# Attention with fp32 products with v, the last 64 keys mixed once, and odd scores copied by VectorE

## The chip, the core and the metric

The kernel runs on one core of a Trainium2 chip. Its time is the device time of one execution in microseconds (us). Before the change three runs gave a median of 881.18 us (880.06 to 882.84). One more execution was profiled; it took 882.68 us, and all rows below are from it.

## The reference

Attention for 4 batches, 12 heads, 448 positions and head size 64 is mixed over heads twice, before and after the softmax; two gated dense blocks follow, which the change does not touch.

```
scores = q @ k.T / sqrt(64)
scores = einsum('bhij,hg->bgij', scores, w_pre)      # heads mixed: premix
attn = exp(scores - max); attn /= sum + 1e-9
attn = einsum('bhij,hg->bgij', attn, w_post)         # heads mixed: postmix
x = attn @ v                                         # then moe, then moe2
```

## The kernel before

Attention comes first and the dense part after it; all instructions of an engine run in the order in which the program lists them, and the loop in `attention` (L438) writes that order by hand.

**Tiles and steps.** The 448 queries of a batch are cut into tiles of 120, 120, 120 and 88. A block is 10 queries of all 12 heads, that is 120 rows, laid out in two halves of the 128 partitions, five queries in each half. A step r takes two blocks; the tile of 88 ends with an odd step of one block of 8 queries. There are 23 steps a batch and 92 in all.

**What a step lists.** `relayout` (L230) copies scores into block layout by DMA on SP's queue, four steps ahead. `postmix(r)` (L288) multiplies the exponentials of the step by the weights `wr`, on tiles of 64x64 of the array: for each block e, each of four groups of 128 keys, both halves of the keys and both halves h of the rows. The keys are 448, so the fourth group overlaps the third by 64 keys. `recip2` and `weigh` (L267, L274) prepare the weights of step r+1 on VectorE and GpSimd. `at_hi` (L319, ScalarE) and `at_lo` (L327, VectorE) split the mixed result in PSUM into two fp16 parts `ah` and `al` for each block. Then come `scores` for a later tile (L202), `premix(r+2)`, its row maximum on VectorE, its exponential on ScalarE and a sum's reciprocal (L238 to L265), then `at_lo` of the second block, and then the step's unit of `attn_v` (L339), when there is one, and `out_x` (L357), which moves a finished half tile out of PSUM for `store_x`.

**The products with v.** `attn_v(b, t, c)` makes one pair of heads for one tile of queries. It sums twelve fp16 terms for each of the two heads: for four groups of keys, v high by `ah`, v high by `al` and v low by `ah`. A tile has six such units, one a step in most steps; two share a step once for the first tile and once for the third tile of each batch, and three share each of two steps for the last tile.

**Preparing v.** v is loaded in four parts a batch (`load_v`). VectorE takes its largest magnitude for each head pair (`v_max`, `v_join`), two small products on TensorE spread it over the partitions (`v_turn`, `v_spread`, which use the scores' PSUM tile psA), VectorE makes a power of two from it (`v_scale`), GpSimd multiplies (`v_mul`), VectorE casts to fp16 (`v_hi`) and GpSimd subtracts to get the low part (`v_lo`), one head pair a step over six steps. `out_x` multiplies by the inverse scale.

**PSUM.** psA is one tile of two banks for scores, psB two banks for premix, psC three banks for postmix and, for odd c of the first two tiles (`apart`, L209), for scores; psD is one bank for attn_v.

Between these, 18 jobs that decode the first dense weight (L575 to L628) put work on ScalarE, VectorE and GpSimd in steps 8 to 85, in the lists `mid` and `late` of the loop.

Of the kernel before, what the change touches and what calls it, by code (L numbers as in the profile page):

```python
# [17 lines left out]
NP = H // 2  # L18
# [3 lines left out]
TB = 8  # L22
# [4 lines left out]
QCOLS = [p + NP * n for p, (t0, n) in zip(SKIP, TILES)]  # L27
LR, LQ = 4, 2
# [3 lines left out]
EXP_BITS = 0x7F800000  # L32


def attention(tc, nc, io, xT, B, extra, tail):
# [16 lines left out]
    with ExitStack() as es:  # L52
# [21 lines left out]
        vsc_p = pool("a_vsc", 2)  # L74
# [4 lines left out]
        def pow2(out_scale, out_inv, mx, n):  # L79

            nc.vector.tensor_scalar(out=mx, in0=mx, scalar1=2.0 ** -100, scalar2=None, op0=ALU.max)
            e = sm_p.tile([128, n], F32, tag="p2e", name="p2e", bufs=1)
            f = sm_p.tile([128, n], F32, tag="p2f", name="p2f", bufs=1)
            nc.vector.tensor_scalar(out=e.bitcast(I32), in0=mx.bitcast(I32), scalar1=EXP_BITS,
                                    scalar2=None, op0=ALU.bitwise_and)
            nc.vector.tensor_scalar(out=f.bitcast(I32), in0=e.bitcast(I32), scalar1=EXP_BITS,
                                    scalar2=None, op0=ALU.bitwise_xor)
            nc.vector.tensor_scalar(out=out_scale, in0=f, scalar1=2.0 ** 13, scalar2=None, op0=ALU.mult)
            nc.vector.tensor_scalar(out=out_inv, in0=e, scalar1=2.0 ** -14, scalar2=None, op0=ALU.mult)

# [8 lines left out]
        KINDS = (SQ, TB)  # L99
        wts = {n: cp.tile([128, H, n], F32, name=f"w{n}") for n in KINDS}  # L100
# [3 lines left out]
        dwp = cp.tile([128, NP], F32, name="dwp")  # L104
        ident = cp.tile([128, 128], F32, name="ident")
        ones = cp.tile([NP, 128], F32, name="ones")

        def consts():
            o = 0
            for n in KINDS:  # L110
                nc.sync.dma_start(out=wts[n], in_=io["kpost"][:, H * o:H * (o + n)].rearrange("p (g i) -> p g i", g=H))
                o += n
            nc.sync.dma_start(out=ident, in_=io["ident"])
            nc.vector.memset(ones, 1.0)
            wrep = e_p.tile([128, S], F32, tag="e", name="wrep")[:, :H * H].rearrange("p (g h) -> p g h", g=H)
            nc.sync.dma_start(out=wrep, in_=io["w_postT"].rearrange("g h -> (g h)").partition_broadcast(128)
                                .rearrange("p (g h) -> p g h", g=H))
            mx = sm_p.tile([128, H], F32, tag="wmx", name="wmx", bufs=1)
            nc.vector.tensor_reduce(out=mx, in_=wrep, axis=AX.X, op=ALU.max, apply_absolute_value=True)
            sw = sm_p.tile([128, H], F32, tag="sw", name="sw", bufs=1)  # L120
            dw = sm_p.tile([128, H], F32, tag="dw", name="dw", bufs=1)
            pow2(sw, dw, mx, H)
            for n in KINDS:
                nc.vector.tensor_tensor(out=wts[n], in0=wts[n], in1=sw.unsqueeze(2).to_broadcast([128, H, n]),
                                        op=ALU.mult)
            for e in range(2):
                nc.vector.tensor_scalar(out=dwp[64 * e:64 * e + 64], in0=dw[64 * e:64 * e + 64, e::2],
                                        scalar1=8.0, scalar2=None, op0=ALU.mult)


        raws, kt, qt = {}, {}, {}
# [10 lines left out]
        vt, dsc = {}, {}  # L142

        vraw = vr_p.tile([128, 4, NP, 128], F32, name="vraw")
        nc.gpsimd.memset(vraw[:64, 3], 0.0)

        def load_v(b, j):
            p = slice(0 if j < 3 else 64, 128)
            nc.sync.dma_start(out=vraw[p, j], in_=io["vN"][b, 128 * j:min(128 * j + 128, S)].rearrange("p (c d) -> p c d", d=128))

        def v_max(b, j):
            if j == 0:
                raws["vmx", b] = sm_p.tile([128, 4, NP], F32, tag="vmx", name="vmx", bufs=1)
            nc.vector.tensor_reduce(out=raws["vmx", b][:, j], in_=vraw[:, j], axis=AX.X, op=ALU.max,
                                    apply_absolute_value=True)

        def v_join(b):
            mx = raws["vmx", b]
            m = raws["vmx", b] = sm_p.tile([128, NP], F32, tag="vmj", name="vmj", bufs=1)
            nc.vector.tensor_reduce(out=m, in_=mx.rearrange("p j c -> p c j"), axis=AX.X, op=ALU.max)  # L160

        def v_turn(b):

            ps = raws["vps", b] = psA.tile([128, 2, 512], F32, tag="psA", name="psV")[:, 0]
            nc.tensor.matmul(ps[:NP, :128], raws.pop(("vmx", b)), ident, start=True, stop=True)

        def v_top(b):
            m = sm_p.tile([NP, 1], F32, tag="vtop", name="vtop", bufs=1)
            nc.vector.tensor_reduce(out=m, in_=raws.pop(("vps", b))[:NP, :128], axis=AX.X, op=ALU.max)
            dg = raws["dg", b] = sm_p.tile([NP, NP], F32, tag="dg", name="dg", bufs=1)  # L170
            nc.vector.tensor_scalar(out=dg, in0=ident[:NP, :NP], scalar1=m, scalar2=None, op0=ALU.mult)

        def v_spread(b):

            ps = raws["vps", b] = psA.tile([128, 2, 512], F32, tag="psA", name="psV")[:, 0]
            nc.tensor.matmul(ps[:, :NP], ones, raws.pop(("dg", b)), start=True, stop=True)

        def v_scale(b):
            mx, dv = (sm_p.tile([128, NP], F32, tag=t, name=t, bufs=1) for t in ("vm", "dv"))
            nc.vector.tensor_copy(mx, raws.pop(("vps", b))[:, :NP])  # L180
            sv = raws["sv", b] = vsc_p.tile([128, NP], F32, tag="sv", name="sv")
            pow2(sv, dv, mx, NP)
            dsc[b] = vsc_p.tile([128, NP], F32, tag="dsc", name="dsc")
            nc.vector.tensor_tensor(out=dsc[b], in0=dv, in1=dwp, op=ALU.mult)

        def v_mul(b, c):
            raw = vraw[:, :, c]
            nc.gpsimd.tensor_scalar(out=raw, in0=raw, scalar1=raws["sv", b][:, c:c + 1], scalar2=0.0,  # L188
                                    op0=ALU.mult, op1=ALU.add)

        def v_hi(b, c):
            vt[b, c] = [v_p.tile([128, 4, 128], F16, tag=f"{t}{c}", name=t) for t in ("vh", "vl")]
            nc.vector.tensor_copy(vt[b, c][0], vraw[:, :, c])

        def v_lo(b, c):
            vh, vl = vt[b, c]
            nc.gpsimd.tensor_tensor(out=vl, in0=vraw[:, :, c], in1=vh, op=ALU.subtract)  # L197
# [4 lines left out]
        def scores(b, t, c):  # L202
# [58 lines left out]
        def recip(r):  # L261
            m, sm = len(ex[r]), rec[r]
            rc = rec[r] = sm_p.tile([128, 2], F32, tag="rc", name="rc")
            nc.gpsimd.tensor_scalar(out=rc[:, :m], in0=sm[:, :m], scalar1=1e-9, scalar2=2.0 ** -14,  # L264
                                    op0=ALU.add, op1=ALU.mult)  # L265
# [5 lines left out]
        def kind(r):  # L271
            return SQ if pairs[r][4] == 2 else pairs[r][5]

        def weigh(r):  # L274
            n, rc = kind(r), rec.pop(r)
            wr[r] = []
            for e in range(len(ex[r])):
                w = wr_p.tile([128, H, IB], F32, tag="wr", name="wr")
                w = w.rearrange("p g i -> p (g i)")[:, :H * n].rearrange("p (g i) -> p g i", i=n)
                nc.gpsimd.tensor_scalar(out=w, in0=wts[n], scalar1=rc[:, e:e + 1], scalar2=0.0,  # L280
                                        op0=ALU.mult, op1=ALU.add)
                wr[r].append(w)

        def keys(x, jc):
            j0 = min(128 * jc, S - 128)
            return x[:, j0:j0 + 128]

        def postmix(r):  # L288
            n = kind(r)
            pc[r] = [psC.tile([128, 4, H, IB], F32, tag="psC", name="psC") for _ in ex[r]]  # L290
            if n != SQ:
                for ps, x, w in zip(pc[r], ex[r], wr[r]):
                    for jc in range(4):
                        nc.tensor.matmul(ps[:, jc, :, :n], keys(x, jc), w, start=(jc == 0), stop=(jc == 3))
# [1030 lines left out]
```

## Time and profile before

| | us |
|---|---|
| median of three runs | 881.18 |
| profiled execution | 882.68 |
| its span | 880.9 |
| TensorE (PE) busy in the span | 847.7 |
| VectorE (DVE) busy | 659.0 |
| ScalarE (ACT) busy | 534.7 |
| GpSimd (POOL) busy | 253.4 |

Busy time is a sum over stages with different limits, and TensorE's products are pipelined, so that their recorded durations overlap. What a product costs is read from the distance to the start of the next one. The granted clock of TensorE was full (2.4 GHz) but for the first microseconds: 0.997 over the span.

### The profile page before, as it was taken

The numbers are of one execution on the slowest core, as the hardware profiler recorded it, in microseconds if no ns is written. First come the engines' busy times: TensorE is split into PE (matmuls) and PEld (weight loads), VectorE is DVE, ScalarE is ACT, GpSimd is POOL, SyncE is SP. The second block draws the span as 40 slices with busy tenths as digits, with TensorE's granted clock in tenths as the row PEclk, the third lists the DMA queues.
The fourth block names the chain that finished last, engine by engine and source line by source line (L and its number), as shares of the span: only waits on it lengthen the run. The fifth ranks groups of instructions, "written<-read, shape, count | busy, mean of one in ns | idle before, by whom it ended". The sixth has DMA issues, their size and how long they took to land.

```text
span 880.9 us, 29335 instructions
## 1 busy us (share of the span) xinstructions
PE 847.7 (96%) x12008; PEld 672.5 (76%) x12008; DVE 659.0 (75%) x1471; ACT 534.7 (61%) x1202; POOL 253.4 (29%) x453
## 2 busy tenths in 40 slices
PE   8898899989999999999999999999999999999998
PEld 2455556656666666788998989898999999999997
DVE  3787888888889888879999998969886368338221
ACT  5788788978898898865656857327535136115010
POOL 0173146224522452100000000017417128306321
PEclk9999999999999999999999999999999999999999
DMA  6566555765576554652585957997530311310301
GB/s 206 171 202 207 166 168 189 236 183 168 175 244 188 161 176 145 183 162 83 155 270 169 295 170 227 326 331 239 193 110 12 115 36 37 115 28 1 108 19 63
DMA packets 108998, 141.70 MB, mean 161 GB/s; under 512 B 25792, under 2 KB 95168, under 8 KB 108864
## 3 DMA queue, kind: packets, MB, share of 16 engines
q1 hardware_dynamic: 108864, 139.82, 50.1%
q8 instruction: 95, 1.56, 0.7%
q14 instruction: 39, 0.32, 0.1%
HBM read 73.66 MB, written 27.59 MB: 115 GB/s over the span
## 4 chain that ended last, share of the span: by engine, by line
PE 70%; DVE 11%; ACT 5%; DMA 5%; POOL 4%; issue 4%; SPq 1%; POOLq 0%; ACTq 0%; DVEq 0%
PE ps L554 47%; PE psC L302 7%; PE psB L244 5%; PE psA L219 5%; PE psD L354 5%; POOL vl L197 2%; DMA wth<-wth_d 2%; ACT e L258 1%; ACT s L225 1%; DVE nmx L250 1%; DMA blk<-s 1%; DVE al L331 1%; POOL wr L280 1%; DMA xres<-xT 1%; POOL vraw L188 1%
## 5 line engine op out<-in xcount | busy, mean ns | idle before, releaser
L258 ACT ACTIVATE e<-psB,nmx 128x448 f32<-128x448 f32 x180 | 112.9, 636 | 36.2 <-DVE nmx L250 35.5
L331 DVE SCALAR_TENSOR_TENSOR al<-psC,ah 128x480 f16<-128x480 f32 x180 | 116.0, 645 | 13.0 <-ACT ah L325 12.1
L302 PE MATMUL psC<-wr,e 64*64 64x60 f32 x5632 | 107.2, 222 | 12.0 <-issue 9.1
L250 DVE TENSOR_REDUCE nmx<-psB 128x1 f32<-128x448 f32 x180 | 103.7, 616 | 17.8 <-PE psB L244 16.2
L302 PEld LDWEIGHTS psC<-wr,e 64*64 64x64 f32 x5632 | 94.0, 135 | 25.5 <-issue 11.4
L550 POOL TENSOR_TENSOR x2s<-x,x2s 128x384 fp32r<-128x384 f32 x28 | 28.8, 1047 | 283.1 <-DMA x2T<-xres 207.9
L244 PE MATMUL psB<-blk,kpre 64*64 64x448 f32 x720 | 102.9, 548 | 1.6 <-DMA blk<-s 0.8
L554 PE MATMUL ps<-wtok,z 128*128 128x448 f32 x504 | 104.3, 367 | 0.0
L325 ACT ACTIVATE ah<-psC 128x480 f16<-128x480 f32 x180 | 93.7, 579 | 15.6 <-PE psC L302 15.3
L554 PEld LDWEIGHTS ps<-wtok,z 128*128 128x128 f32 x504 | 94.6, 188 | 9.0
L219 PE MATMUL psA<-k,q 64*64 64x448 f32 (+2 forms) x768 | 94.4, 545 | 6.2 <-ACT s L225 5.2
L354 PEld LDWEIGHTS <-vh 128*64 128x64 f16 x1536 | 56.4, 110 | 56.9 <-issue 56.7
L554 PE MATMUL ps<-wth,x2s 128*128 128x384 f32 x504 | 94.2, 342 | 2.5 <-POOL x2s L550 1.9
L554 PEld LDWEIGHTS ps<-wth,x2s 128*128 128x128 f32 x504 | 88.1, 188 | 4.1 <-POOL x2s L550 2.9
L554 PE MATMUL ps<-u,wch 128*128 128x448 f32 x432 | 89.5, 367 | 0.0
L225 ACT ACTIVATE s<-psA 124x896 f32<-124x896 f32 (+1 forms) x90 | 84.1, 935 | 8.7 <-PE psA L219 5.9
L554 PEld LDWEIGHTS ps<-u,wch 128*128 128x128 f32 x432 | 81.1, 188 | 7.6
L550 POOL TENSOR_TENSOR z<-zz,z 128x384 fp32r<-128x384 f32 x56 | 64.3, 1169 | 55.7 <-ACT z L547 55.6
L547 ACT ACTIVATE u<-xres 128x448 fp32r<-128x448 f32 x24 | 13.8, 577 | 98.8 <-DVE xres L1133 98.8
L264 POOL TENSOR_SCALAR rc<-sum 128x2 f32<-128x2 f32 (+1 forms) x92 | 22.3, 243 | 174.2 <-ACT e L258 173.0
L244 PEld LDWEIGHTS psB<-blk,kpre 64*64 64x64 f32 x720 | 37.2, 132 | 44.5 <-issue 22.3
L280 POOL TENSOR_SCALAR wr<-w,rc 128x60 f32<-128x60 f32 x180 | 54.2, 314 | 55.6 <-DVE rc L269 45.2
(133 smaller groups left out, 1610.0 us busy)
## 6 DMA issues: line engine op xcount, KB each, us to landing
blk<-s SPq DMA_DIRECT2D x176, 210.0 KB
draw<-in_w_in SPq DMA_DIRECT2D x24, 256.0 KB
k<-in_kvT SPq DMA_DIRECT2D x24, 224.0 KB
xraw<-xT SPq DMA_DIRECT2D x24, 224.0 KB
xres<-xT SPq DMA_DIRECT2D x24, 224.0 KB
x2T<-xres SPq DMA_DIRECT2D x24, 224.0 KB
xres<-x2T SPq DMA_DIRECT2D x24, 224.0 KB
out<-uu SPq DMA_DIRECT2D x24, 224.0 KB
```

The source lines that it names most:

```text
L219: nc.tensor.matmul(ps[e][r, :S], q[p, o + r.start:o + r.stop], k[p], start=True, stop=True)
L225: nc.scalar.activation(out=out, in_=pair[:m, :, :S], func=AF.Copy, scale=0.125)
L244: nc.tensor.matmul(ps[e][c:c + 64, :S], kpre[k, e], blk[k], start=True, stop=True)
L250: nc.vector.tensor_reduce(out=nmx[r][:, e:e + 1], in_=ps[:, :S], axis=AX.X, op=ALU.max, negate=True)
L258: nc.scalar.activation(out=x, in_=ps[:, :S], func=AF.Exp, bias=m[:, e:e + 1], accum_out=sm[:, e:e + 1])
L280: nc.gpsimd.tensor_scalar(out=w, in0=wts[n], scalar1=rc[:, e:e + 1], scalar2=0.0, op0=ALU.mult, op1=ALU.add)
L302: nc.tensor.matmul(pc[r][h][c:c + 64, jc, :, SQ * e:SQ * e + SQ], x[p, c:c + 64], wr[r][e][p], start=(e == 0 and jc == 0), stop=(e == 1 an ...
L325: nc.scalar.activation(out=at_view(r, e, at[b, t][0]), in_=at_src(r, e), func=AF.Copy, scale=2.0 ** -17)
L331: nc.vector.scalar_tensor_tensor(out=al, in0=at_src(r, e), scalar=2.0 ** -17, in1=ah, op0=ALU.mult, op1=ALU.subtract)
L354: nc.tensor.matmul(ps[p, o:o + n], v[:, jc, p], a[:, i0:i0 + n], start=(o == 0 and m == 0), stop=(o > TI and m == len(terms) - 1))
L550: eng.tensor_tensor(out=out, in0=in_, in1=hi.bitcast(F32), op=ALU.subtract)
L554: self.nc.tensor.matmul(ps, l, r, start=(i == 0), stop=(i == len(terms) - 1))
```

## The change

v is no longer split, scaled or cast. `vt` holds two fp32 copies of v, one for even and one for odd batches, loaded by DMA alone; the fourth part, 64 keys, is loaded into both halves of the partitions. The maxima, the scales, the two small products, the casts and the constants that they needed are gone.

`postmix` runs over three groups of 128 keys, and the last 64 keys are mixed once, block 0 into the lower and block 1 into the upper half of the partitions. The odd step uses the same tiles of 64x64 in place of the whole array. The result is copied out in fp32 (`at_copy`): bank h = 0 by ScalarE, bank h = 1 by VectorE, 84 x 5 = 420 columns each. psC has two banks and psD two.

`attn_v` makes, for each head, three fp32 products over 128 keys and then the last 64 keys on tiles of 64x64, the lower half into one bank and the upper half into the other. `out_x` copies one and adds the other, with three more small instructions for the tile of 88.

For the first two tiles the odd scores are copied by VectorE instead of ScalarE. v's loads move: for the first batch to steps 1 to 4, for others to 14, 11, 8 and 5 steps before the batch's first step.

```diff
-        psC = pool("psC", 3, space=PSUM)
-        psD = pool("psD", 1, space=PSUM)
+        psC = pool("psC", 2, space=PSUM)
+        psD = pool("psD", 2, space=PSUM)
...
+        vt = [p.tile([128, 4, NP, 128], F32, tag="v", name="v") for p in (vr_p, v_p)]
         def load_v(b, j):
...
+            src = io["vN"][b, 128 * j:min(128 * j + 128, S)].rearrange("p (c d) -> p c d", d=128)
+            for p in (slice(0, 128),) if j < 3 else (slice(0, 64), slice(64, 128)):
+                nc.sync.dma_start(out=vt[b % 2][p, j], in_=src)
...
             if apart:
                 for e in range(2):
-                    nc.scalar.activation(out=out[:, e], in_=ps[e][:m, :S], func=AF.Copy, scale=0.125)
+                    nc.vector.tensor_scalar(out=out[:, e], in0=ps[e][:m, :S], scalar1=0.125, scalar2=None,
+                                            op0=ALU.mult)
...
         def postmix(r):
...
+            pc[r] = [psC.tile([128, AX3, SQ], F32, tag="psC", name="psC") for _ in range(2)]
+            two = len(ex[r]) == 2
+            for e, (x, w) in enumerate(zip(ex[r], wr[r])):
+                for jc in range(3):
+                    for c in (0, 64):
                         for h in range(2):
                             p = slice(64 * h, 64 * h + 64)
+                            o = (3 * (e if two else h) + jc) * H
+                            nc.tensor.matmul(pc[r][h][c:c + 64, o:o + H], x[p, 128 * jc + c:128 * jc + c + 64], w[p],
+                                             start=(e == 0 and jc == 0), stop=(not two and jc == 2 and c != 64 * h))
+            for e in range(2):
+                for h in range(2) if two else (e,):
+                    p, i = slice(64 * h, 64 * h + 64), e if two else 0
+                    nc.tensor.matmul(pc[r][h][64 * e:64 * e + 64, AM:], ex[r][i][p, 384:], wr[r][i][p],
+                                     start=False, stop=True)
...
+        def at_copy(r, h):
...
+            copy = nc.vector.tensor_copy if h else nc.scalar.copy
+            if m == 2:
+                copy(a[:, :, k + h], pc[r][h])
                 return
...
         def attn_v(b, t, c):
...
+            halves = [slice(64 * e, 64 * e + 64) for e in range(2)]
+            for jc in range(3):
+                for i, p in enumerate(halves):
+                    nc.tensor.matmul(ps[p], v[:, jc, p], main[:, H * jc + 2 * c + i],
+                                     start=(o == 0 and jc == 0), stop=False)
+            for e, q in enumerate(halves):
+                for i, p in enumerate(halves):
+                    nc.tensor.matmul(px[p] if e else ps[p, 0], v[q, 3, p], rest[q, 2 * c + i],
+                                     start=(o == 0 and e == 1), stop=(o > TI))
...
+            for j in range(4):
+                put(early, f - 14 + 3 * j if b else 1 + j, load_v, b, j)
...
             if live:
-                at_hi(r, 0)
-                at_lo(r, 0)
-                at_hi(r, 1)
+                at_copy(r, 0)
+                at_copy(r, 1)
...
-            if live:
-                at_lo(r, 1)
```

## Rows read from the trace of the kernel before

**Rows 1.** The page's part 1: busy us of each engine, share, instructions.
```profile
PE 847.7 (96%) x12008; PEld 672.5 (76%) x12008; DVE 659.0 (75%) x1471; ACT 534.7 (61%) x1202; POOL 253.4 (29%) x453
```

**Rows 2.** Busy time by stretch, all engines: stretch, length, busy us (instructions), PE's clock, DMA.
```profile
120.00:180.00 60.00, 57.83 (x1713) 36.58 (x1706) 51.55 (x118) 54.09 (x128) 27.38 (x65) 1.00 0.63 202
...
380.00:880.00 500.00, 494.06 (x2483) 452.69 (x2482) 350.30 (x762) 222.08 (x479) 119.44 (x108) 1.00 0.45 142
```

**Rows 3.** Timeline of PE, steps from 249.97: start, us, line, count.
```profile
249.97 1.16 PE L302 MATMUL psC<-wr,e 64*64 64x60 f32 x64
250.95 0.93 PE L219 MATMUL psA<-k,q 64*64 64x448 f32 x8
251.71 0.93 PE L244 MATMUL psB<-blk,kpre 64*64 64x448 f32 x8
252.56 0.24 PE L354 MATMUL psD<-ah,vh 128*64 128x120 f16 x2
...
253.31 1.16 PE L302 MATMUL psC<-wr,e 64*64 64x60 f32 x64
...
258.57 1.16 PE L302 MATMUL psC<-wr,e 64*64 64x60 f32 x64
```

**Rows 4.** Stretches, postmix alone (64 a step): length, PE busy (count), PEld busy (count).
```profile
110.38:148.27 37.89, 10.78 (x576) 9.57 (x576) 1.00 0.52 170
198.24:236.53 38.29, 10.72 (x576) 9.52 (x576) 1.00 0.51 167
284.44:322.51 38.07, 11.13 (x577) 9.65 (x577) 1.00 0.50 164
48.56:69.23 20.67, 6.12 (x320) 5.44 (x320) 1.00 0.65 215
236.53:253.31 16.78, 5.79 (x320) 5.12 (x320) 1.00 0.72 234
339.42:355.17 15.75, 5.79 (x320) 5.12 (x320) 1.00 0.48 131
```

**Rows 5.** Timeline of PE at the odd step: its product and the next.
```profile
284.44 1.13 PE L294 MATMUL psC<-wr,e 128*128 128x96 f32 x8
285.50 0.60 PE L219 MATMUL psA<-k,q 64*64 64x448 f32 x4
```

**Rows 6.** Timeline of PE, postmix of two steps with units 88 wide.
```profile
119.27 1.16 PE L302 MATMUL psC<-wr,e 64*64 64x60 f32 x64
...
122.46 0.75 PE L302 MATMUL psC<-wr,e 64*64 64x60 f32 x36
```

**Rows 7.** Groups by shape, the whole run: count | busy us, mean ns | idle before.
```profile
L197 POOL TENSOR_TENSOR vl<-vraw,vh 128x512 f16<-128x512 f32 x24 | 27.9, 1164 | 0.0
...
L193 DVE CAST vh<-vraw 128x512 f16<-128x512 f32 x24 | 12.8, 532 | 7.1 <-POOL vraw L188 7.1
L362 DVE TENSOR_TENSOR x<-psD,dsc 128x360 f32<-128x360 f32 x24 | 12.6, 524 | 3.4 <-PE psD L354 3.1 <-DMA xT<-x 0.4
```

**Rows 8.** Waits from 60 to 340 us: total us, times, longest.
```profile
PE psC L302 <- issue: 9.1, 9, 2.4
```

**Rows 9.** Timeline of ScalarE and VectorE in the step from 249.97.
```profile
251.32 1.04 ACT L325 ACTIVATE ah<-psC 128x480 f16<-128x480 f32 x2
...
251.74 0.17 DVE L269 RECIPROCAL rc<-rc 128x2 f32<-128x2 f32 x1 [0.67 <-POOL rc L264]
251.92 0.66 DVE L331 SCALAR_TENSOR_TENSOR al<-psC,ah 128x480 f16<-128x480 f32 x1
...
252.69 1.15 DVE L250 TENSOR_REDUCE nmx<-psB 128x1 f32<-128x448 f32 x2
...
253.76 0.65 DVE L331 SCALAR_TENSOR_TENSOR al<-psC,ah 128x480 f16<-128x480 f32 x1
```

**Rows 10.** Timeline of PE at the start, scores, with the idle time before.
```profile
7.26 1.73 PE L219 MATMUL psA<-k,q 64*64 64x448 f32 x16 [0.28 <-ACT s L225]
9.28 1.73 PE L219 MATMUL psA<-k,q 64*64 64x448 f32 x16 [0.29 <-ACT s L225]
```

More of the change, by code (lines that the diff above doesn't have):

```diff
@@ L21 @@
 SQ = 5
-TB = 8
 TI = IB * 12
@@ L27 @@
 QCOLS = [p + NP * n for p, (t0, n) in zip(SKIP, TILES)]
+AW = [-(-n // IB) * SQ for t0, n in TILES]
+AM, AX3 = 2 * 3 * H, 2 * 3 * H + H
 LR, LQ = 4, 2
@@ L98, in attention @@
         kpre = cp.tile([128, 2, 64], F32, name="kpre")
-        KINDS = (SQ, TB)
-        wts = {n: cp.tile([128, H, n], F32, name=f"w{n}") for n in KINDS}
+        wts = cp.tile([128, H, SQ], F32, name="wts")
         blks = [cp.tile([128, S], F32, name=f"blk{i}") for i in range(6)]
@@ L103, in attention @@
             nc.vector.memset(blk, 0.0)
-        dwp = cp.tile([128, NP], F32, name="dwp")
-        ident = cp.tile([128, 128], F32, name="ident")
-        ones = cp.tile([NP, 128], F32, name="ones")
         def consts():
[L109 to L131, printed above, removed]
+            nc.sync.dma_start(out=wts, in_=io["kpost"].rearrange("p (g i) -> p g i", g=H))
+        kt, qt = {}, {}
         def load_k(b, c):
@@ L151, in v_max @@
[L151 to L197, printed above, removed]
+            src = io["vN"][b, 128 * j:min(128 * j + 128, S)].rearrange("p (c d) -> p c d", d=128)
@@ L281, in weigh @@
                                         op0=ALU.mult, op1=ALU.add)
                 wr[r].append(w)
-        def keys(x, jc):
-            j0 = min(128 * jc, S - 128)
-            return x[:, j0:j0 + 128]
         def postmix(r):
[L289 to L294, printed above, removed]
-                return
-            for e in range(2):
-                for jc in range(4):
-                    x = keys(ex[r][e], jc)
-                    for c in range(0, 128, 64):
+            pc[r] = [psC.tile([128, AX3, SQ], F32, tag="psC", name="psC") for _ in range(2)]
@@ L316, in at_src @@
-        def at_src(r, e):
-            return pc[r][e].rearrange("p c g i -> p (c g) i")[:, :, :pairs[r][5]]
-        def at_hi(r, e):
-            b, t = pairs[r][:2]
-            if e >= len(pc[r]):
-                return
-            if r == first[b, t] and e == 0:
-                at[b, t] = [at_p.tile([128, 4 * H * TI], F16, tag=tag, name=tag) for tag in ("ah", "al")]
-            nc.scalar.activation(out=at_view(r, e, at[b, t][0]), in_=at_src(r, e), func=AF.Copy, scale=2.0 ** -17)
-        def at_lo(r, e):
-            if e >= len(pc[r]):
-                return
-            ah, al = (at_view(r, e, x) for x in at[pairs[r][:2]])
-            nc.vector.scalar_tensor_tensor(out=al, in0=at_src(r, e), scalar=2.0 ** -17, in1=ah,
-                                           op0=ALU.mult, op1=ALU.subtract)
+            if r == first[b, t] and h == 0:
+                at[b, t] = at_p.tile([128, AX3 * max(AW)], F32, tag="at", name="at")
@@ L341, in attn_v @@
-            ah, al = at[b, t]
-            vh, vl = vt[b, c]
+            w, a, v = AW[t], at[b, t], vt[b % 2][:, :, c]
             if c % 3 == 0:
-                acc[b, t] = psD.tile([128, 512], F32, tag="psD", name="psD", bufs=1)
-            ps = acc[b, t]
-            terms = []
-            for jc in range(4):
-                terms += [(vh, jc, ah), (vh, jc, al), (vl, jc, ah)]
-            o = TI * (c % 3)
-            for m, (v, jc, a) in enumerate(terms):
-                for e in range(2):
-                    p = slice(64 * e, 64 * e + 64)
-                    i0 = (jc * H + 2 * c + e) * n
-                    nc.tensor.matmul(ps[p, o:o + n], v[:, jc, p], a[:, i0:i0 + n],
-                                     start=(o == 0 and m == 0), stop=(o > TI and m == len(terms) - 1))
@@ L357, in out_x @@
-        def out_x(b, t, half):
-            n = TILES[t][1]
-            ps = acc.pop((b, t))[:, :3 * TI].rearrange("p (j i) -> p j i", i=TI)[:, :, :n]
-            x = xs[b, t, half] = x_p.tile([128, 3, TI], F32, tag=f"x{half}", name="x")
-            sc = dsc[b][:, 3 * half:3 * half + 3].unsqueeze(2).to_broadcast([128, 3, n])
-            nc.vector.tensor_tensor(out=x[:, :, :n], in0=ps, in1=sc, op=ALU.mult)
+                acc[b, t] = [psD.tile([128, 512], F32, tag="psD", name="psD") for _ in range(2)]
@@ new lines, in attn_v @@
+            ps, px = acc[b, t]
+            o = TI * (c % 3)
+            ps = ps[:, o:o + 2 * w].rearrange("p (k e s) -> p e k s", e=2, s=SQ)
+            px = px[:, o // 2:o // 2 + w].rearrange("p (k s) -> p k s", s=SQ)
+            main = a[:, :AM * w].rearrange("p (e x k s) -> p x e k s", e=2, x=3 * H, s=SQ)
+            rest = a[:, AM * w:AX3 * w].rearrange("p (x k s) -> p x k s", x=H, s=SQ)
+            halves = [slice(64 * e, 64 * e + 64) for e in range(2)]
[3 more added lines that the diff above has]
+                                     start=(o == 0 and jc == 0), stop=False)
@@ new lines, in attn_v, with out_x @@
+            for e, q in enumerate(halves):
+                for i, p in enumerate(halves):
+                    nc.tensor.matmul(px[p] if e else ps[p, 0], v[q, 3, p], rest[q, 2 * c + i],
+                                     start=(o == 0 and e == 1), stop=(o > TI))
+        def out_x(b, t, half):
+            w, nb = AW[t] // SQ, TILES[t][1] // IB
+            ps, px = (p[:, :m * TI // 2].rearrange("p (j k e s) -> p j k e s", j=3, e=f, s=SQ)
+                      for p, m, f in zip(acc.pop((b, t)), (6, 3), (2, 1)))
+            x = xs[b, t, half] = x_p.tile([128, 3, TI], F32, tag=f"x{half}", name="x")
+            y = x.rearrange("p j (k e s) -> p j k e s", e=2, s=SQ)
+            nc.vector.tensor_copy(y[:, :, :nb], ps[:, :, :nb])
+            add = [(y[:, :, :nb, 1], px[:, :, :nb, 0])]
+            if w > nb:
+                m = SQ - 1
+                z = x[:, :, IB * nb:IB * nb + 2 * m].rearrange("p j (e s) -> p j e s", s=m)
+                for e in range(2):
+                    nc.vector.tensor_copy(z[:, :, e], ps[:, :, nb, e, 1 - e:SQ - e])
+                add.append((z[:, :, 1], px[:, :, nb, 0, :m]))
+            for a, b in add:
+                nc.vector.tensor_tensor(out=a, in0=b, in1=a, op=ALU.add)
@@ L390, in attention @@
             f = first[b, 0]
-            z = f - 1 if b else 3
-            for j, d in enumerate((8, 7, 5, 4) if b else (5, 4, 3, 2)):
-                put(early, z - d, load_v, b, j)
-                put(late, z - d + 2 if b else min(z - d + 2, z - 1), v_max, b, j)
-            put(late, z - 1, v_join, b)
-            put(work, z, v_turn, b)
-            put(late, z, v_top, b)
-            put(work, z + 1, v_spread, b)
-            put(late, z + 1, v_scale, b)
-            for c in range(NP):
-                put(mid, z + 2 + c, v_mul, b, c)
-                put(late, z + 2 + c, v_hi, b, c)
-                put(mid, z + 3 + c, v_lo, b, c)
+            for j in range(4):
+                put(early, f - 14 + 3 * j if b else 1 + j, load_v, b, j)
         for T in range(nt):
@@ L1273, in layout @@
     kpre = np.zeros((2, 64, 2, 64), np.float32)
-    kinds = [np.zeros((2, 64, H, n), np.float32) for n in (SQ, TB)]
+    kpost = np.zeros((2, 64, H, SQ), np.float32)
     for x in range(SQ):
@@ L1280, in layout @@
             kpre[r, p, 1, o1:o1 + H] = i["w_pre"]
[L1281 to L1285 removed]
+            kpost[r, p, :, x] = i["w_post"]
     vN = v.transpose(0, 2, 1, 3).reshape(B, S, DM)
```

48 lines of the change are left out of this document (9 added, 39 removed).

## The prediction

> **What bounds the kernel now.** I read the page's first part, then the busy times by stage, then the timeline of one ordinary step of attention, then the length of the steps, stretch by stretch.
>
> The span is 880.9 us; the profiled execution took 882.68 us and the median of the three timed runs is 881.18 us, so I make the sum against 882.68 and take 1.5 us off at the end. PE is busy nearly throughout [rows 1]. From 380 us on, PE is busy 494 of 500 us [rows 2]: that is the dense part, which the diff leaves alone. So only the first 375 us can move, and there PE, ScalarE and VectorE are all near full [rows 2].
>
> In an ordinary step PE goes from product to product: postmix (L302) at 249.97, scores (L219) 0.98 later, premix (L244) 0.76 after that, attn_v (L354) 0.85 after that, the next postmix 0.75 later: 3.34 us, set by PE [rows 3]. Five such steps in a row take 16.78 us, 3.356 each [rows 4]. The steps of v's preparation are longer: ten steps take 37.89, 38.29 and 38.07 us [rows 4]. What PE alone wants there is 4.07 (the odd product 1.06, scores 0.76, premix 0.85, two units of attn_v 1.40) [rows 3, 5] + 6 x 3.19 (units 88 columns wide, 119.27 to 122.46) [rows 6] + 3 x 3.34 = 33.23, so 4.7, 5.1 and 4.8 us are waits. For the first batch the five steps from 48.56 take 20.67 us [rows 4] against 4 x 3.34 + 3.99 = 17.35: 3.3 more.
>
> **The change, part by part.** An fp32 product shows as two passes: postmix has 32 calls and 64 records, attn_v in fp16 24 calls and 24 records. Passes on different tiles of the array run together; I call such a set a round.
>
> *Postmix.* Now 64 passes in 16 rounds of four 64x64 tiles take 0.98 us, 0.061 a round [rows 3]. After: 24 calls for three blocks of keys and 4 for the last 64, so 14 rounds: -0.12 a step, x 88 = -10.8 us. The odd step's 8 passes on the whole array take 285.50 - 284.44 = 1.06 us [rows 5]; after, 12 + 2 calls in 6 + 2 rounds are 0.49: 4 x -0.57 = -2.3.
>
> *attn_v.* Now 24 passes in 12 rounds of two take 0.75 us [rows 3], of which I give 0.10 to the change of the tiles' shape: premix has the scores' two rounds of 448 columns, and yet attn_v starts 0.85 after it, not 0.76. That leaves 0.054 a round. After: 6 calls, 12 passes, 6 rounds of two with 120 columns in fp32; then 4 calls on 64x64 tiles with 60 columns, two rounds of four. No row shows fp32 on 128x64 tiles. From below: scores stream 448 columns in 0.76 / 2 = 0.38 a round [rows 3], which gives 0.102 for 120. From above: the odd product, 1.06 / 8 for 96 columns [rows 5], gives 0.166 for 120. I take 0.102 + 0.010 = 0.112, as postmix's rounds are 0.010 above the scores' rate (0.051 for 60), and its stationary blocks too are 64 columns wide. Then 6 x 0.112 + 0.10 for the change of shape, now inside the unit, + 2 x 0.061 = 0.89, +0.14 a unit, x 96 = +13.4 (ends +8 and +45). Where units share a step (one more unit for the first tile, one for the third of each batch, four for the last: nine) the shape changes back and forth once more, 2 x 0.10: +1.8.
>
> PE's own work is then +2.1 us: no faster.
>
> The Trainium skill (TensorE: Matmul & The Clock Gate, LDWEIGHTS) says that a weight load takes its columns divided by 1.2 per ns, whatever the rows. By that rule the odd product is held by its 128-column loads (estimate 107 ns of the 0.13) and not by its columns; loads of 64 columns would take 53 ns, under the streaming time, which favours the low end. Its sum would be 0.102 a round, 6 us less than mine. No run here separates load from stream.
>
> *What v's preparation held up.* It removes 24 VectorE casts of 0.53, 24 GpSimd subtractions of 1.16 [rows 7], the multiplications, four maxima a batch and two small products a batch that borrow the scores' only PSUM pair. Of the 4.7 + 5.1 + 4.8 + 3.3 = 17.9 us found above I leave 3.9 to the weight decoding that shares these steps and to PE's waits for "issue" [rows 8]: -14.0. Bounds: 0, if decoding alone causes them, to -17.9.
>
> *ScalarE and VectorE.* Each step loses one ScalarE copy (two take 1.04 now) and two VectorE subtractions of 0.65, and gains one VectorE copy of 420 elements, about 0.57 by length [rows 9]. out_x grows: 0.52 for 360 elements [rows 7], and after it an addition of half as many, about 0.33; four small ones more for the narrow tile. That is some 14 us of VectorE in all; its cover is PE's step, and VectorE loses 0.73 a step. Without cover it would cost at most those 14. What the relief returns: steps with two units of scores: the one from 253.31 to 258.57 takes 5.26 [rows 3], where PE wants 3.34 + 0.76; there are three, and I take half of that wait from each, -1.8; the 0.016 by which an ordinary step is over 3.34, x 90, -1.5; steps without scores, 3.15 each [rows 4], bound by the loop premix, row maximum (1.15) [rows 9], exponential, premix; there a subtraction of 0.65 becomes a copy of 0.57, -0.1 each: -1.0. Bounds for the three: 0 to -7.
>
> *psC with two buffers.* Postmix fills both, so the next one waits for both copies. Today the second subtraction starts at 253.76 and ends 4.44 after its postmix began [rows 3, 9], hence three buffers. After, VectorE's copy stands right behind the reciprocal, which ends at 251.91: done by 252.5, 0.8 before the next postmix at 253.31. ScalarE's starts at 251.32 [rows 9]. Cost 0; late is only what exceeds 0.8. Behind the waiting postmix all of PE would stand.
>
> *Start.* Even scores share one PSUM pair: 7.26 to 9.28, two calls in 2.02 us, each ending in a wait for ScalarE [rows 10]. That loop, an even product and ScalarE's copy of it, stays when VectorE takes the odd ones: 0 until 14 us. Later v's loads leave the steps where the first blocks are laid out, and the small products go: -2.5 (0 to -5). On SP's queue v's loads are moved to steps 1 to 4, and for later batches to 14, 11, 8 and 5 steps ahead, with one DMA more a batch; the second buffer keeps them from waiting. Cost 0, at most one step's transfer.
>
> Sum: +2.1 - 14.0 - 4.3 - 2.5 = -18.7; 882.7 - 18.7 = 864.0, less 1.5: about **863 us**.
>
> **Rivals.** *Strided writes.* attn_v's output now goes in runs of five columns. Postmix writes such runs already, at 0.061 for 60 columns [rows 3]; if its 0.010 over the scores' rate is a price per column and doubles in a longer pass, a round is 0.125 to 0.13: +0.10 a unit, 96 x 0.10 = 10 us more, 873. For it: the runs; against: 0.010 is small and can be a price per round. The Trainium skill (PSUM — Partial Sum Buffer, Specifications) states that any non-contiguous pattern slows matmuls significantly; the trace's 0.061 against 0.051 agrees at most weakly.
>
> *fp32 at the odd product's rate.* At 0.166 a round a unit costs +0.47, 45 us in place of 13.4: 864 + 32 = 896, less 1.5: 894, slower. It decides from about 0.145 a round, where 96 x 6 x 0.033 eats the 18.7. For it: the only fp32 row with 128 rows in use; against: its stationary block is twice as wide.
>
> *Hidden work.* The waits of v's steps are the decoding's, and only PE's +2.1, -2.5 at the start and a few copies stay: 878 to 880. For it: decoding jobs lie in these stretches too; against: they lie in the ordinary stretch as well, which runs at 3.356 a step [rows 4].
>
> *Two psC buffers too few.* If VectorE's copy comes 1.1 late (0.3 past its slack), 88 x 0.3 = 26: 889. Against: VectorE loses work ahead of it.
>
> *More goes.* PE's waits for "issue" in postmix, 9.1 us in nine places [rows 8], go too, since passes fall from 104 to 92 a step: 854.
>
> **How the numbers follow.** Forecast 0.54 (856 to 869 its own range), strided 0.13, hidden work 0.12, odd product's rate 0.10, more goes 0.06, psC 0.05. Runs of this kernel can't tell less than 0.3%, 2.6 us. Faster, under 878.5: 0.54 + 0.13 + 0.06 and a third of the hidden work, 0.77; same: the rest of that, 0.08; slower 0.15. The range 853 to 879 leaves out the slow cases and half of the last ones.
>
> **What would show it.** Right: steps of 3.3 to 3.4 us in the stretches where ten took 38; a unit of attn_v near 0.89 with its main rounds near 0.11; postmix to scores 0.86; ScalarE and VectorE clearly under PE; VectorE's copy ended before the next postmix. Wrong: PE's wait at postmix put down to a copy; main rounds of 0.14 or more; long steps that stay where v was prepared.

## The result, and the profile after

The kernel after takes 866.14 us (median of four runs, 864.76 to 868.35) against 880.62 us before (four, 876.37 to 882.84): ratio 0.984, 95% interval 0.980 to 0.989. A second comparison (six runs against 17) gave 0.988 (0.985 to 0.990). The prediction was 863; the time lies 3 us above it, inside the range of its likeliest case (856 to 869). The profiled execution took 866.24 us, 16.4 less than the one of before.

The page's first part [rows 1], and the first stretch of [rows 2] in the kernel after (the same columns):

```profile
PE 842.7 (97%) x10984; PEld 664.9 (77%) x10984; DVE 592.1 (68%) x1364; ACT 493.6 (57%) x1106; POOL 204.6 (24%) x404
```

```profile
120.00:180.00 60.00, 55.75 (x1407) 34.41 (x1400) 36.88 (x92) 44.14 (x102) 15.31 (x51) 0.94 0.66 197
```

VectorE has lost 67 us of work and ScalarE 41, and PE 5. In this stretch VectorE fell from 51.55 to 36.88, yet PE too is less busy than before (55.75 for 57.83) and its granted clock is 0.94 for 1.00: something new holds it there.

PE's timeline of the ordinary step from 251.91 [rows 3], and of the odd step from 268.95 [rows 5]:

```profile
251.91 0.88 PE L201 MATMUL psC<-wr,e 64*64 64x60 f32 x48
252.61 0.30 PE L206 MATMUL psC<-wr,e 64*64 64x60 f32 x8
252.72 0.94 PE L130 MATMUL psA<-k,q 64*64 64x448 f32 x8
253.48 0.93 PE L156 MATMUL psB<-blk,kpre 64*64 64x448 f32 x8
254.34 0.84 PE L242 MATMUL psD<-at,v 128*64 128x120 f32 x12
255.11 0.34 PE L246 MATMUL psD<-at,v 64*64 64x60 f32 x8
...
268.95 0.53 PE L201 MATMUL psC<-wr,e 64*64 64x60 f32 x24
...
269.31 0.58 PE L130 MATMUL psA<-k,q 64*60 64x448 f32 x2
```

From start to start: postmix 0.81, scores 0.76, premix 0.86, attn_v's main part 0.77, the rest 0.16 until the next postmix at 255.27: 3.36 us, as before, with the work moved from postmix (0.98) to attn_v (0.93 for 0.75). In the odd step the scores start 0.36 after postmix, where it was 1.06.

The stretches of [rows 4] that held v's preparation, postmix's main products alone (L201, without those of the last 64 keys; the same columns):

```profile
100.76:134.59 33.83, 8.59 (x456) 7.61 (x460) 1.00 0.57 183
187.87:221.88 34.01, 8.58 (x456) 7.61 (x460) 1.00 0.59 192
268.95:302.99 34.04, 8.90 (x456) 7.80 (x460) 1.00 0.56 186
44.78:63.85 19.07, 4.45 (x241) 4.04 (x244) 1.00 0.69 218
```

37.89, 38.29, 38.07 and 20.67 became 33.83, 34.01, 34.04 and 19.07: together 14.0 us less. Read with [rows 4], the borders of these stretches give the rest. The first comes 3.8 us earlier (44.78 for 48.56). Between the first and the second it is 36.91 for 41.15, between the third and the last 47.07 for 47.91, but between the second and the third 53.28 for 49.97: there 3.3 us were lost. In the stretch that became 36.91 three of PE's waits for "issue", 4.2 us in all, stood before; now they are 0.2 us. By the last step's postmix (343.58 for 363.33 on PE's timeline) 19.75 us are gained. Of these, 3.3 us are gone at the end; most of them (2.4 by the start of the third group of dense products) where the last six units stand three in a row between dense products.

Where the 3.3 us of the middle went: PE, ScalarE and SP's queue from 152.26 in the kernel after (in brackets the idle time before and what ended it), and the same stretch by windows (all engines, as in [rows 2]):

```profile
152.26 0.88 PE L201 MATMUL psC<-wr,e 64*64 64x60 f32 x48
...
153.19 4.40 SPq L148 DMA_DIRECT2D blk<-s  x4
...
158.04 0.92 ACT L137 ACTIVATE s<-psA 124x896 f32<-124x896 f32 x1 [4.11 <-DMA blk<-s]
...
159.01 1.76 PE L130 MATMUL psA<-k,q 64*64 64x448 f32 x8 [4.25 <-ACT s L137]
...
162.37 0.86 PE L201 MATMUL psC<-wr,e 64*64 64x60 f32 x24
```

```profile
140.00:152.00 12.00, 12.00 (x296) 7.23 (x288) 8.60 (x22) 9.68 (x22) 3.68 (x12) 1.00 0.92 260
...
156.00:160.00 4.00, 0.98 (x8) 0.29 (x8) 0.00 (x0) 1.96 (x4) 0.00 (x0) 0.72 0.67 233
160.00:164.00 4.00, 4.00 (x88) 2.99 (x84) 1.23 (x4) 1.75 (x5) 0.19 (x1) 0.50 0.48 142
```

This step with two units of scores takes 10.11 us. The three of its kind, in order, took 5.88, 4.89 and 5.26 before and 5.63, 10.11 and 6.51 after. The first copy of the scores waits 4.11 us for transfers that still read the tile of scores it is to overwrite; the second product waits for the copy. DMA was 0.92 busy in the twelve microseconds before (0.79 from 153 to 165 us in the kernel before, ahead of the same step): v's loads, put 14 and 11 steps ahead, now fall among k's. And PE's clock is granted at 0.72 in the mean of the stretch with the pause and at 0.50 (1.2 GHz) in the next, so the next scores take 1.76 where they take 0.94 in the step from 251.91.

Last, PE's waits from 60 to 340 us that bear on the case [rows 8]:

```profile
PE psA L130 <- ACT s L137: 7.7, 3, 4.3
...
PE psC L201 <- issue: 1.1, 3, 0.6
```

The waits for "issue" in postmix fell from 9.1 us to 1.1 (3.2 in a second profile of the same kernel, shown with the last experiment); no wait of postmix for a copy has come.

### The profile page after: what moved, and what is told of

It is laid out like the page before. It is cut to its first block, busy times and chain, and to the rows that moved or that the text cites. A ratio compares the mean times of both kernels' runs of the same rounds, so it can differ in the third digit from the quotient of the medians.

```text
span 864.5 us, 27167 instructions
## 1 busy us (share of the span) xinstructions
PE 842.7 (97%) x10984; PEld 664.9 (77%) x10984; DVE 592.1 (68%) x1364; ACT 493.6 (57%) x1106; POOL 204.6 (24%) x404
## 4 chain that ended last, share of the span: by engine, by line
PE 91%; issue 3%; DMA 2%; DVE 2%; ACT 1%; POOL 0%; ACTq 0%; POOLq 0%; DVEq 0%; SPq 0%
PE ps L442 55%; PE psB L156 8%; PE psD L242 8%; PE psA L130 8%; PE psC L201 7%; PE psD L246 3%; DMA blk<-s 2%; PE psC L206 1%; PE ps L960 1%; DMA x<-x2T 1%; ACT s L137 0%; ACT e L170 0%; DVE s L134 0%; POOL x2s L438 0%; POOL z L438 0%
## 5 line engine op out<-in xcount | busy, mean ns | idle before, releaser
L242 PEld LDWEIGHTS psD<-at,v 128*64 128x64 f32 x1152 | 56.5, 137 | 60.6 <-issue 39.9
L156 PE MATMUL psB<-blk,kpre 64*64 64x448 f32 x720 | 97.9, 541 | 1.9 <-DMA blk<-s 1.1
L201 PE MATMUL psC<-wr,e 64*64 64x60 f32 x4320 | 83.4, 220 | 1.7 <-issue 1.1
L201 PEld LDWEIGHTS psC<-wr,e 64*64 64x64 f32 x4320 | 74.1, 136 | 8.6 <-POOL wr L188 5.3
L242 PE MATMUL psD<-at,v 128*64 128x120 f32 (+1 forms) x1152 | 77.3, 269 | 0.0
L176 POOL TENSOR_SCALAR rc<-sum 128x2 f32<-128x2 f32 (+1 forms) x92 | 17.9, 195 | 210.5 <-ACT e L170 210.5
L188 POOL TENSOR_SCALAR wr<-wts,rc 128x60 f32<-128x60 f32 x180 | 54.1, 314 | 48.1 <-DVE rc L181 36.5
L442 PE MATMUL ps<-slot,x 128*128 128x512 f32 x252 | 60.1, 396 | 0.0
```

Source lines behind the costliest of these rows:

```text
L156: nc.tensor.matmul(ps[e][c:c + 64, :S], kpre[k, e], blk[k], start=True, stop=True)
L188: nc.gpsimd.tensor_scalar(out=w, in0=wts, scalar1=rc[:, e:e + 1], scalar2=0.0, op0=ALU.mult, op1=ALU.add)
L201: nc.tensor.matmul(pc[r][h][c:c + 64, o:o + H], x[p, 128 * jc + c:128 * jc + c + 64], w[p], start=(e == 0 and jc == 0), stop=(not two and ...
L242: nc.tensor.matmul(ps[p], v[:, jc, p], main[:, H * jc + 2 * c + i], start=(o == 0 and jc == 0), stop=False)
L442: self.nc.tensor.matmul(ps, l, r, start=(i == 0), stop=(i == len(terms) - 1))
```

## The experiments

All ratios are to the kernel before, run beside on the same chip; its medians there were 876.81 to 878.59 us. So kernels are compared by their ratios, 1% being 8.8 us.

### What v's preparation cost, in the kernel before

```
-            vh, vl = vt[b, c]
+            vh, vl = vt[0, c]
...
-                put(late, z - d + 2 if b else min(z - d + 2, z - 1), v_max, b, j)
+                if not b:
+                    put(late, min(z - d + 2, z - 1), v_max, b, j)
+            if b:
+                continue
             put(late, z - 1, v_join, b)
```

> The kernel before, in which v is prepared for the first batch only: the maxima, the small products, the multiplications, casts and subtractions of batches 2 to 4 are left out and these batches multiply with the first one's parts; v's loads, attn_v and the decoding stay. By my prediction's step (the waits of v's steps go with its preparation: 4.7, 5.1 and 4.8 us in the three stretches of ten steps, less what the decoding keeps) the stretches of 37.89, 38.29 and 38.07 us fall to about 34, and the time by 11 to 14 us: ratio 0.984 to 0.988. Rival, hidden work: the waits are the decoding's, the stretches stay near 38 and the time within 3 us.

Measured 865.37 us, ratio 0.988 (0.985 to 0.990): for three of the four batches, this work alone is worth nearly what the whole change gains. The three stretches of ten steps (columns of [rows 4]):

```profile
103.38:137.72 34.34, 10.61 (x577) 9.40 (x577) 1.00 0.57 187
186.92:221.65 34.73, 10.86 (x576) 9.52 (x576) 1.00 0.55 181
268.56:302.88 34.32, 10.74 (x577) 9.40 (x577) 1.00 0.54 183
```

3.55, 3.56 and 3.75 us less than in [rows 4], 10.9 in sum, though v's loads and the decoding stayed and postmix and attn_v are the old ones. The hidden-work rival falls. Two more things in this profile bear on what follows. PE has as many passes a step as in the kernel before, and yet its waits for issue in postmix (columns of [rows 8]) are 3.2 us and not 9.1:

```profile
PE psC L302 <- issue: 3.2, 7, 1.1
```

And its first seven steps, which the edit leaves alone, end 2.2 us earlier than in the profile of before (46.32 for 48.56): so far can two profiles of the same start lie apart.

### Odd scores back to ScalarE

```
-                    nc.vector.tensor_scalar(out=out[:, e], in0=ps[e][:m, :S], scalar1=0.125, ...)
+                    nc.scalar.activation(out=out[:, e], in_=ps[e][:m, :S], func=AF.Copy, scale=0.125)
```

> One part undone: the odd products' scores of the first batch's first two tiles go back to ScalarE. I predicted that VectorE's taking them gives nothing at the start, since the even products borrow one PSUM pair and set the loop: 865 to 867, first step of attention at the same time within 0.3 us. Rival: it is this part that brings step 7 forward by 3.9 us (predicted 2.5 from v's preparation): then 868 to 870, with step 0 or step 7 some 2 to 4 us later.

866.50 us, 0.987 (0.985 to 0.988): no difference that these runs can show. The first premix comes at 14.86 in place of 15.11 and the tenth at 45.45 in place of 46.43. VectorE's copies gain nothing at the start that can be seen; the microsecond that they seem to lose is less than two profiles of one start differ by.

### Sums written contiguously

```
-            ps = ps[:, o:o + 2 * w].rearrange("p (k e s) -> p e k s", e=2, s=SQ)
+            ps = ps[:, o:o + TI].rearrange("p (e k s) -> p e k s", e=2, s=SQ)[:, :, :w // SQ]
```

> attn_v writes its main sums as two runs of sixty columns, one for each parity of the queries, in place of runs of five in turn; out_x then reads them apart (one copy more). If runs of five cost TensorE nothing, main rounds stay at 0.102 to 0.103 us and the time at 865 to 868 (out_x's extra copy is hidden). If each column of a short run had a price, rounds would fall below 0.102 and the longer first round (0.153) would shrink too: by 0.01 a round 96 x 6 x 0.01 = 6 us less, 860.

871.69 us, 0.992 (0.991 to 0.993). PE in an ordinary step of this kernel:

```profile
231.43 0.93 PE L156 MATMUL psB<-blk,kpre 64*64 64x448 f32 x8
232.29 0.84 PE L242 MATMUL psD<-at,v 128*64 128x120 f32 x12
233.06 0.34 PE L246 MATMUL psD<-at,v 64*64 64x60 f32 x8
233.22 0.47 PE L201 MATMUL psC<-wr,e 64*64 64x60 f32 x20
```

0.86, 0.77, 0.16: to the hundredth what the runs of five gave, and single main rounds stand 0.102 us apart in both. Strided writes cost TensorE nothing here. I had expected no change of the time; it is 4 to 7 us over the kernel after's two ratios. The profiled run took 868.24 and shows its long steps where the kernel after has them (8.84, 9.75 us); why the other four lie above it stays open.

### v's loads elsewhere

First at the old steps, then late and spaced (one of the two lines that are added):

```
-                put(early, f - 14 + 3 * j if b else 1 + j, load_v, b, j)
+                put(early, f - (9, 8, 6, 5)[j] if b else 1 + j, load_v, b, j)
+                put(early, f - 8 + 3 * j if b else 1 + j, load_v, b, j)
```

> v's loads of the later batches go back to the steps they had before the change, 9, 8, 6 and 5 ahead of the batch's first step, behind k's loads in place of among them; the rest is the kernel after. My theory: after the change v's loads fall on k's, and the transfers that lay out the blocks for the two-unit score steps come late, which costs some 8 us (the step from 152.26 takes 10.11 us where 5.25 would do, the one from 238.68 takes 6.51, two neighbours 0.8 and 1.0 too much). With the loads apart these go: about 858 us, no scores' wait for ScalarE over 3 us left. Rival 1: k's loads alone hold the blocks up, and v's place does not matter: 866, the same long steps. Rival 2: PE's waits for issue in postmix (9.1 us before the change, 1.1 after) come from v's loads beside the decoding's, and return with the old places: the 8 us gained are given back, 864 to 867, with waits for issue of 5 us or more.

> v's loads of the later batches three steps apart from 8 steps ahead of the batch's first step to one behind it (its first use is six steps behind it). By my theory as good as the old places or better, 857 to 859: no load of k beside them, and never two loads of v in neighbouring steps. If the pace of v's loads and not their coming with k's is what matters, this is clearly better than the old places (by 2 us or more); if k's loads alone hold the blocks up, 866.

861.16 us, 0.981 (0.979 to 0.984), at the old steps, 3 us over what was expected; 858.55 us, 0.978 (0.976 to 0.979), spaced. PE's waits for the scores' copy, of the spaced kernel and with the columns of [rows 8]:

```profile
PE psA L130 <- ACT s L137: 3.6, 3, 2.1
```

7.7 us became 3.6 (3.7 at the old steps), the longest 4.3 became 2.1, and the granted clock stays at 1.00 over the whole run. No wait for issue of PE in postmix over 0.2 us is left in the spaced kernel; at the old steps there are 1.2 us, so rival 2 falls. A lead of 2 us or more was to be the sign that the pace of v's loads matters too. The spaced loads are ahead by 2.6 us, but the two intervals just touch, so that stays open.

### The two units in another step, and with the loads spaced

```
-            return [lo + (c * (hi - lo + 1)) // NP for c in range(NP)]
+            return [lo + (c * (hi - lo + 1) + 3) // NP for c in range(NP)]
```

> In the kernel after, the score tile of six units that has only five steps takes its two units in the fourth step in place of the first. My theory: the long steps (10.11, 6.51, 5.63 us) are long because the tile's first copy waits until the tile of scores before the last is out, and the second product of the same step stands behind that copy on the one PSUM pair and holds all of PE. Elsewhere the copy's wait stays but PE goes on: the two-unit steps take 4.1 to 4.3, some 8 to 10 us less, ratio to before 0.973 to 0.976. Rival: DMA is full there and the blocks come late whatever the order; the wait moves to premix or to the next scores, and the time stays at 0.984.

> v's loads spaced and the two units in the fourth step, attn_v as in the kernel after. Alone the first gave 0.9775 and the second 0.9836, where its profiled run still has waits of 4.2 and 1.9 us in two neighbouring steps of the second batch, put down to transfers. If these are v's loads on k's, the two edits add up: 5 to 8 us below the first alone, ratio 0.968 to 0.972. If the long steps are the same loss seen twice: 0.975 to 0.979.

Alone 862.89 us, 0.984 (0.981 to 0.986): nothing gained that can be told, the rival was right. ScalarE and PE in the step that was to be freed:

```profile
157.94 0.92 ACT L137 ACTIVATE s<-psA 124x896 f32<-124x896 f32 x1 [5.10 <-DMA blk<-s]
...
158.91 0.98 PE L130 MATMUL psA<-k,q 64*64 64x448 f32 x8 [2.96 <-ACT s L137]
160.20 0.28 PEld L156 LDWEIGHTS psB<-blk,kpre 64*64 64x64 f32 x2 [1.09 <-ACT e L170]
```

The copy waits for the transfers longer still (5.10 us for 4.11), and in ScalarE's order the exponentials stand behind it: the wait goes to the next scores and to premix. With the loads spaced too: 857.58 us, 0.977 (0.975 to 0.979), PE's waits for the copy down to 0.9 us, but no faster than spacing alone. It is the same loss seen twice, and v's loads among k's bring it: moving them takes most of it away, moving the units does not. The kernels with spaced loads are the fastest of all that were run, ahead of both kernels compared here.

### What the change of tiles costs, and waits for issue

attn_v's main products on 64x64 tiles, the halves of the keys into two banks that out_x adds:

```
-                for i, p in enumerate(halves):
-                    nc.tensor.matmul(ps[p], v[:, jc, p], main[:, H * jc + 2 * c + i],
...
+                for acc_e, q in zip((ps, px), halves):
+                    for i, p in enumerate(halves):
+                        nc.tensor.matmul(acc_e[p], v[q, jc, p], main[q, H * jc + 2 * c + i],
```

> attn_v's main products too on 64x64 tiles: each half of 128 keys by itself, the two halves of the keys into two PSUM banks that out_x adds; 16 calls a unit in place of 10, in rounds of four, and no change of the tiles' shape is left in a step. My theory: of a unit's 0.93 us 0.15 is the change of shape (first round 0.153 in place of 0.102, 0.195 from the last main round to the rest), so a unit takes 6 x 0.102 to 0.112 + 2 x 0.06 = 0.73 to 0.79, the ordinary step 3.17 to 3.22, and the time falls by 96 x 0.14 to 0.20 less what the loop of 3.15 us keeps: 10 to 16 us below the kernel after, ratio to before 0.966 to 0.974. Rival 1: the 0.15 is the price of passes over 128 rows, and the smaller tiles stream no faster together: no gain, 0.984. Rival 2: passes a step go from 92 back to 104 and PE's waits for issue return with them (8 us before): 0.975 to 0.982 with such waits of 6 us or more.

873.51 us, 0.996 (0.993 to 0.999): slower than the kernel after by 7 to 10 us. Its step on PE's timeline, where nothing waits:

```profile
79.33 0.93 PE L156 MATMUL psB<-blk,kpre 64*64 64x448 f32 x8
80.09 0.79 PE L243 MATMUL psD<-at,v 64*64 64x120 f32 x24
80.70 0.28 PE L247 MATMUL psD<-at,v 64*64 64x60 f32 x8
80.81 0.87 PE L201 MATMUL psC<-wr,e 64*64 64x60 f32 x48
...
81.63 0.93 PE L130 MATMUL psA<-k,q 64*64 64x448 f32 x8
82.39 0.66 PE L156 MATMUL psB<-blk,kpre 64*64 64x448 f32 x4
```

3.06 us for 3.36: premix 0.76 for 0.86, main part 0.61 for 0.77, rest 0.11 for 0.16. So the two changes of the tiles' shape cost 0.31 us a step, and rival 1 falls. But PE now waits for its instructions:

```profile
PE psC L201 <- issue: 9.6, 14, 1.4
...
PE psC L206 <- issue: 3.3, 3, 1.6
```

and many steps take 3.1 to 4.9 us. Rival 2 was right in kind and undersized. Two such waits, and PE's records between them:

```profile
122.72 0.50 PE L201 MATMUL psC<-wr,e 64*64 64x60 f32 x17 [0.82 <-issue]
123.00 0.33 PE L206 MATMUL psC<-wr,e 64*64 64x60 f32 x8
123.12 0.97 PE L130 MATMUL psA<-k,q 64*64 64x448 f32 x8
123.88 0.96 PE L156 MATMUL psB<-blk,kpre 64*64 64x448 f32 x8
124.63 0.68 PE L243 MATMUL psD<-at,v 64*64 64x90 f32 x24
125.09 0.27 PE L247 MATMUL psD<-at,v 64*64 64x45 f32 x7
125.18 0.24 PE L201 MATMUL psC<-wr,e 64*64 64x60 f32 x1
125.19 0.22 PE L247 MATMUL psD<-at,v 64*64 64x45 f32 x1
125.19 0.93 PE L201 MATMUL psC<-wr,e 64*64 64x60 f32 x47
125.90 0.28 PE L206 MATMUL psC<-wr,e 64*64 64x60 f32 x5
127.78 0.27 PE L206 MATMUL psC<-wr,e 64*64 64x60 f32 x2 [1.59 <-issue]
```

17 + 8 + 8 + 8 + 24 + 7 + 1 + 1 + 47 + 5 = 126 passes. The part of the page on the DMA queues has, for this kernel,

```profile
q8 instruction: 96, 1.57, 0.7%
```

96 packets for this kernel's 12136 passes, 126 to a packet; in the kernels before, after and the next one it is 95 for 12008, 87 for 10984 and 99 for 12472. The wait stands in the middle of a product, at the border of two packets. Counted through the whole trace, all 27 of PE's waits for issue in this kernel stand a multiple of 126 passes apart, to within three, and each ends 1.2 to 1.7 us after a packet of this queue has landed. Why a packet comes late no run here shows. To tell the number of passes from the shape of the work, the scores' and premix's products of the kernel after were cut in two:

```
+            for j in (slice(0, S // 2), slice(S // 2, S)):
...
-                    nc.tensor.matmul(ps[e][r, :S], q[p, o + r.start:o + r.stop], k[p], start=True, stop=True)
...
+                        nc.tensor.matmul(ps[e][r, j], q[p, o + r.start:o + r.stop], k[p, j], start=True, stop=True)
```

> The kernel after with each of the scores' and premix's products of 448 columns cut into two of 224: the same columns, tiles and shapes, 16 passes a step more (92 to 108). My theory of PE's waits for issue: the instructions of 126 passes come in one transfer, and PE waits where a step uses them up faster than the next one lands (104 passes in 3.34 us before: 9.1 us of such waits; 92 in 3.36 after: 1.1; 104 in 3.05 with four tiles: some 15 and more). Then waits for issue of 8 us or more come back here, and the time rises by these and by 8 more rounds' ends a step at 0.01 to 0.03 (0.04 to 0.12 us, 4 to 11 us): ratio 0.997 to 1.008. Rival: the waits of the four tiles come from the shape of their work, not from the number of passes: issue stays at 1 to 3 us, and only the rounds' ends count: 0.988 to 0.997.

880.47 us, 1.003 (1.001 to 1.006), back at the time of before. Steps in which nothing waits stay at 3.37 us, so the 16 passes more, of half the length, cost nothing themselves; the waits are the price:

```profile
PE psC L203 <- issue: 5.2, 8, 1.8
...
PE psC L208 <- issue: 3.0, 7, 0.8
```

With 2.1 us of such waits elsewhere they are 10.3 us, of the size of the 9.2 us by which the profiled run (875.43) lies over that of the kernel after; the other runs mostly lie higher. In postmix there are 15 such waits, 8.2 us, with 108 passes in 3.37 us (32 a us); 17, 12.9 us, with 104 in 3.06 (34, four tiles); 9, 9.1 us, with 104 in 3.34 (31, before), but there too 7 of only 3.2 us without v's preparation; and 3 of 1.1 us and 5 of 3.2 in two profiles with 92 in 3.36 (27, after). So in these profiles the passes per microsecond go with how often PE waits; how long one wait is, they do not tell. The mechanism stood; of the price I had put 4 to 11 us on the ends of rounds, and that part is nothing.

All of it at once, loads spaced, units moved and four tiles:

> Three edits on the kernel after at once: v's loads spaced (alone 0.9775), two units in the fourth step, four tiles in attn_v. The first two take away the same long steps, so not all of both adds up: after 866 less 8 to 11, less 10 to 16: 840 to 848 us, ratio 0.955 to 0.964, ordinary steps near 3.2 us. If the three cover the same loss: 0.972 to 0.978.

873.82 us, 0.996 (0.993 to 0.999): far from the 840 to 848 expected. 11 us of waits for issue stand in postmix's first line alone; spaced loads don't shorten them.

The kernel after once more, beside the last of these:

> The kernel after, unchanged, beside its variants on one chip: ratio to before 0.983 to 0.988 (0.9844 before, and 0.9865 with the one part undone).

867.38 us (860.86 to 870.43), 0.988. PE's waits for issue in its postmix:

```profile
PE psC L201 <- issue: 3.0, 4, 1.1
PE psC L206 <- issue: 0.2, 1, 0.2
```

## Why the prediction was right

The large terms came out as its sum said. Beside them stand two misses of some 8 us each, the waits for issue and v's loads, that cancel; that they do is luck, as nothing ties the one to the other. By the traces +2.1 - 14.0 - 3.8 - 8.0 = -23.7 for PE's work, v's preparation, the start and the waits for issue; 16.4 were gained, so 7.3 were lost, and spaced loads give back 6 to 9.

- **PE's own work, +2.1.** Right in sum: 3.36 us a step was forecast (3.34 - 0.12 + 0.14) and measured. By terms: postmix fell by 0.16 to 0.17 in place of 0.12, and a unit takes 0.93 in place of 0.89. Its main rounds stand at 0.102, the low end, so the rivals of strided writes and of the odd product's rate are wrong. What was mis-sized is the change of the tiles' shape: 0.10 + 0.10 were allowed a step, two changes cost 0.31. The Trainium skill (TensorEngine Tiling (Array Packing), Key Properties) says that a change of tiling mode has to drain the TensorE, and gives no price; the step of 3.06 for 3.36 agrees. On strided writes the Trainium skill (PSUM — Partial Sum Buffer, Specifications) speaks against the change: "any non-contiguous AP slows matmuls significantly". Here a round takes 0.102 us in runs of five and 0.102 written contiguously; the two runs disagree with the page, and the measurement decides.
- **v's preparation, -14.0.** Right in sum and by the stretches named (of waits for issue, only 0.9 us lay in them before); leaving it out of the kernel before gives 10.9 us for three of the four batches.
- **ScalarE and VectorE, -4.3.** Wrong. Steps without scores stay at 3.15 to 3.22, the ordinary step at 3.36. Of the three steps with two units of scores, where I took 0.6 us off each, one fell by 0.25 us and two became longer, to 10.11 and 6.51.
- **v's loads, "cost 0, at most one step's transfer".** This is the step that failed: I counted the queue they stand in and not what else is on its way there. Among k's loads they hold up the transfers of the scores; loads spaced behind k's give back 0.7 to 1.0% (0.978 for 0.984 and 0.988), 6 to 9 us.
- **psC with two buffers, 0.** Right: no wait of postmix for a copy.
- **Start, -2.5.** 3.8 by the trace, but only 1.5 against the other profile of the old start (44.78 for 46.32), so the size is not settled; step 0 stays where it was, as said, and no gain from VectorE's copies shows in it.
- **Waits for issue.** I left them out of the sum and gave their vanishing 0.06, because passes fall from 104 to 92. They fell from 9.1 us to 1.1 and 3.2 in two profiles, and hide the loss at the loads. The reason is shown in part only: cutting products brings the waits back, but without v's preparation they are 3.2 us with 104 passes too.

## What to carry to other kernels

A load that is moved ahead costs what it meets: look at which transfers are on their way at its new place and which wait ends on them. Count matrix passes per microsecond beside their time, since a step that is shorter by PE's work alone can end in waits for instructions. And a relief of engines that do not set the step's end need not return anything: 67 us off VectorE and 41 off ScalarE left the ordinary step at 3.36 us.

## What was unexpected of the hardware

PE's instructions arrive in packets of 126 passes (each a weight load and a product), and the faster a packet is used up (126 / 92 x 3.36 = 4.6 us after, 126 / 104 x 3.34 = 4.05 before, 126 / 104 x 3.06 = 3.7 with four tiles), the more often PE stops at its end: 3, 9 and 17 times in postmix, for 0.8 and 1.6 us in the places shown. Two changes between 64x64 and 128x64 tiles cost 0.31 us a step. After PE's wait of 4.25 us in the step from 152.26 the granted clock was 0.50 from 160 to 164 us, and the scores right behind the wait took 1.76 us for 0.94. Fp32 products of 120 columns stream at 0.102 us a round of two passes on 128x64 tiles and at the same rate in rounds of four on 64x64.
